# A linear-attention and two-MLP kernel with its order set by its own list scheduler: heads on one half of the rows, weight words two tiles at a time, ten token tiles run ahead

## The chip, the cores and the metric

One core of a Trainium2 chip runs the whole program. The metric is the device time of one execution in microseconds, from the first to the last instruction and what lies around them. Engines: PE (TensorE, with its weight loads as PEld), DVE (VectorE), ACT (ScalarE), POOL (GpSimd), and SP, which here only issues transfers.

## The reference

The inputs are `q`, `k`, `v` of (4, 8, 768, 64) in float32. Per batch and head a state of 64x64 decays by gamma and takes up `k v` at each of the 768 positions; the output is the query times the state. The outputs, as 3072 tokens of 512, go through two MLPs. The weights are float64.

```python
for t in range(S):
    state = gamma[None, :, None, None] * state + einsum('bhd,bhe->bhde', k[:, :, t], v[:, :, t])
    y[:, :, t] = scale * einsum('bhd,bhde->bhe', q[:, :, t], state)
x = y.transpose(0, 2, 1, 3).reshape(B * S, H * D)          # (3072, 512)
h = x @ w_in                                               # d_ff 1024
e = exp(h - max(h)); sm = e / (sum(e) + 1e-9); s = h * sm
ln = (s - mean(s)) / sqrt(var(s) + 1e-6) * g_ln
x = ln @ w_out                                             # (3072, 512)
h = x @ w_in2                                              # d_ff 2048
out = (h * cos(h)) @ w_out2
```

## The kernel before

**Attention** runs in 24 steps (two batch pairs of 12 chunks of 64 positions). A step makes one token tile of 128 rows by 512. `score_pair` (lines 230, 231) multiplies keys by queries, `score_mask` (L248) applies the decayed mask in two halves of 64 rows, `state_pair` (L241) adds to the 64x64 states in PSUM, `state_copy` (L255, L256) copies them to SBUF, and `att_out` (L287, L290) multiplies scores and queries, laid one above the other on 128 rows, by values and state, then scales into `x`. Scores and state run with K=64 on quadrants of the array, outputs with K=128 and 64 columns. `att_prep` has POOL scale the mask (L219) and ACT the keys (L223). Each step's loads are six transfers on SP's queue (L91 to L98).

**Words.** A float64 weight is read as two int32 words; `load_w` (L155 to L167) makes a float32 of them, a tile of 128x512 at a time: one ACT operation and four of DVE. `load_w1` and `load_o1` do it for the first MLP, `keep` does it for the second and stores the result (L191), `load_kept` fetches it again (L195). Every matmul operand is split into a high part and a residual (`split`, L125 on ACT, L128 on DVE), and a product is three matmuls.

**First MLP.** Per tile `mm1` (L315) makes two halves of 12 matmuls of 512 columns; `norm` (L323 to L336) does the softmax and the normalization, its small operations on DVE and one power on POOL (L334). Per pair of tiles `transp` (L351) transposes in four groups, with L354 and L355 for high part and residual, and `mm2` (L368) makes 2 x 48 matmuls of 256 columns; its result goes to DRAM (`y1d`).

**Second MLP.** Per block of 512 tokens and per j of 16, `up` (L393) makes 12 matmuls of 512 columns, then ACT and DVE work out `h cos(h)` (L400 to L405, L125, L128), and `down` (L418) adds 12 matmuls into four accumulators, `LAG` = 3 later. L423 copies them out and L427 stores them.

**Order.** PE's order is as written (`manual_schedule` for PE alone); the other engines' order is made by the framework's own timeline. At the start the loads of `w_in`, steps 0 to 3 of the attention and the first halves of `mm1` are interleaved by hand. Then `EARLY` = 2 groups, that is four token tiles, run ahead of the loop over 256-token groups, in which each turn has two tiles of `mm1`, one group of `transp` and `mm2`, attention steps (`att_both`, where scores of step n+1 and state of step n alternate) and some `weights`. Only from that loop on do scores and state alternate; before, they are blocks of their own.

Of the kernel before, what the change touches and what calls it, by code (L numbers as in the profile page):

```python
# [22 lines left out]
C = 64  # L23
# [9 lines left out]
K2 = FF2 // 128  # L33
NG = NT // 256
NBLK = NT // 512
LAG = 3
EARLY = 2
RING = 6
TINY = float(np.array([0x38100000], np.uint32).view(np.float32)[0])
# [8 lines left out]


@with_exitstack  # L50
def body(ctx: ExitStack, tc: tile.TileContext, qx, kt, kn, vn, c_sc, c_mg,
         w_in1, w_out1, gln, w_in2, w_out2, out):
    nc = tc.nc
    pe_order = tc.manual_schedule(engines={mybir.EngineType.PE})
    ctx.enter_context(pe_order)

    const = ctx.enter_context(tc.tile_pool(name="const", bufs=1, side="left"))
    dram = ctx.enter_context(tc.tile_pool(name="dram", bufs=1, space=DRAM))
    p_hp = ctx.enter_context(tc.tile_pool(name="hp", bufs=1, side="right"))
    hp = p_hp.tile([128, 120], F32, name="hp")  # L60
    p_w2a = ctx.enter_context(tc.tile_pool(name="w2a", bufs=1, side="right"))
    stg = ctx.enter_context(tc.tile_pool(name="stg", bufs=2, side="right"))

    y1d = [dram.tile([128, KD, 512], F32, name=f"y1d{n}") for n in range(NBLK)]


    ph1 = ExitStack()
    p_w1 = ctx.enter_context(tc.tile_pool(name="w1", bufs=1, side="left", reuse_waits="tile"))
    p_u = ctx.enter_context(tc.tile_pool(name="u", bufs=2 * EARLY + 2, side="left", reuse_waits="tile"))
    moe = ph1.enter_context(tc.tile_pool(name="moe", bufs=1, side="left", reuse_waits="tile"))  # L70
    boot = ExitStack()
    boot_w = ExitStack()
    p_boot = boot_w.enter_context(tc.tile_pool(name="boot", bufs=1, side="left", reuse_waits="tile"))
    ps1 = ph1.enter_context(tc.tile_pool(name="ps1", bufs=1, side="left", space=PSUM))
    att = ExitStack()
    pa = att.enter_context(tc.tile_pool(name="att", bufs=3, side="right", reuse_waits="tile"))
    psa = att.enter_context(tc.tile_pool(name="psa", bufs=1, side="right", space=PSUM))


    steps = [(bp, i) for bp in range(NB2) for i in range(NI)]  # L80
    st = {}

    def load_step(n):
        bp, i = steps[n]
        d = {}
        d["kt"] = pa.tile([128, 8, C], F32, tag="kt", name="kt", bufs=2)
        d["X"] = pa.tile([128, 2, 8, C], F32, tag="X", name="X")
        d["kn"] = pa.tile([128, NHP, 2 * D], F32, tag="kn", name="kn")
        d["W"] = pa.tile([128, 2, 8, D], F32, tag="W", name="W")
        d["mg"] = pa.tile([128, 2, NHP, C], F32, tag="mg", name="mg", bufs=2)  # L90
        nc.sync.dma_start(out=d["kt"], in_=kt[bp, i].rearrange("p (j s) -> p j s", s=C))  # L91
        src = qx[bp, i].rearrange("p (j s) -> p j s", s=C)
        nc.sync.dma_start(out=d["X"][64:128, 0], in_=src[64:128])
        nc.sync.dma_start(out=d["X"][0:64, 1], in_=src[0:64])
        src = vn[bp, i].rearrange("p (j s) -> p j s", s=D)
        nc.sync.dma_start(out=d["W"][0:64, 0], in_=src[0:64])
        nc.sync.dma_start(out=d["W"][64:128, 1], in_=src[64:128])
        nc.sync.dma_start(out=d["kn"], in_=kn[bp, i].rearrange("p (j s) -> p j s", s=2 * D))  # L98
        if i == 0:
            nc.gpsimd.memset(d["W"][64:128, 0], 0.0)  # L100
            nc.gpsimd.memset(d["W"][0:64, 1], 0.0)
        st[n] = d

    load_step(0)
    mg = const.tile([128, 2, NHP, C], F32, name="mg")
    cs = const.tile([128, 3, NI, NHP], F32, name="cs")
    gcol = const.tile([128, K1], F32, name="gcol")
    nc.scalar.dma_start(out=mg, in_=c_mg.rearrange("p (u a t) -> p u a t", u=2, t=C))
    nc.scalar.dma_start(out=cs, in_=c_sc.rearrange("p (u a t) -> p u a t", u=3, t=NHP))
    nc.scalar.dma_start(out=gcol, in_=gln)  # L110
    mhalf = const.tile([128, 1], F32, name="mhalf")
    nc.gpsimd.memset(mhalf, -0.5)
    nc.gpsimd.memset(hp[:, 0:1], HALFPI)
    sms = [const.tile([128, 16], F32, name=f"sm{n}") for n in range(3)]
    const.tile([128, 16], F32, name="pad")
    ident = const.tile([128, 128], F32, name="ident")
    make_identity(nc, ident)


    w1h = p_w1.tile([128, KD, FF1], F32R, tag="w1h", name="w1h")  # L120
    w1l = p_w1.tile([128, KD, FF1], F32R, tag="w1l", name="w1l")
    o1 = []

    def split(hi, lo, src, pin=False, head=None):
        op = nc.scalar.activation(out=hi, in_=src if head is None else head, func=AF.Copy)  # L125
        if pin:
            tc.keep_in_program_order(op)
        nc.vector.tensor_tensor(out=lo, in0=src, in1=hi.bitcast(F32), op=ALU.subtract)  # L128

    p2 = {}  # L130
    seq = [0]

    early = []

    def fetch_w1(c):
        for k in range(KD):
            raw = p_boot.tile([128, 512, 2], I32, tag="raw", name="raw", bufs=2 * KD)
            nc.sync.dma_start(
                out=raw, in_=w_in1[k * 128:(k + 1) * 128, c * 1024:(c + 1) * 1024].rearrange("p (f two) -> p f two", two=2))
            early.append(raw)  # L140

    def load_w(src, apart=False):
        seq[0] += 1
        if early:
            raw = early.pop(0)
            src = None
            t = p_boot.tile([128, 512], I32, tag="wt", name="wt", bufs=4)
        elif "lt" not in p2 and seq[0] % 2:
            raw = p2["boot"].tile([128, 512, 2], I32, tag="raw", name="raw", bufs=3)
            t = p2["boot"].tile([128, 512], I32, tag="wt", name="wt", bufs=2)  # L150
        else:
            raw = stg.tile([128, 512, 2], I32, tag="raw", name="raw", bufs=3)
            t = stg.tile([128, 512], I32, tag="wt", name="wt")
        if src is not None:
            nc.sync.dma_start(out=raw, in_=src.rearrange("p (f two) -> p f two", two=2))  # L155
        f = t.bitcast(F32)
        top, low = raw[:, :, 1], raw[:, :, 0]
        first_op = nc.scalar.activation(out=f, in_=top.bitcast(F32), func=AF.Abs)
        if seq[0] > 2 * KD:
            tc.keep_in_program_order(first_op)  # L160
        nc.vector.tensor_scalar(out=f, in0=f, scalar1=TINY, scalar2=HUGE, op0=ALU.max, op1=ALU.min)  # L161
        nc.vector.tensor_scalar(out=t, in0=t, scalar1=3, scalar2=0x3FFFFFFF,  # L162
                                op0=ALU.logical_shift_left, op1=ALU.bitwise_and)
        nc.vector.scalar_tensor_tensor(out=t, in0=top, scalar=-0x40000000, in1=t,  # L164
                                       op0=ALU.bitwise_and, op1=ALU.bitwise_or)
        full = low if apart else t
        nc.vector.scalar_tensor_tensor(out=full, in0=low, scalar=29, in1=t,  # L167
                                       op0=ALU.logical_shift_right, op1=ALU.bitwise_or)
        return (f, full.bitcast(F32)) if apart else f

    w_in1, w_out1, w_in2, w_out2 = (w.bitcast(I32) for w in (w_in1, w_out1, w_in2, w_out2))

    def load_w1(k, c):
        head, t = load_w(w_in1[k * 128:(k + 1) * 128, c * 1024:(c + 1) * 1024], True)
        cs = slice(c * 512, (c + 1) * 512)
        split(w1h[:, k, cs], w1l[:, k, cs], t, head=head)

    def load_o1(j):
        head, t = load_w(w_out1[j * 128:(j + 1) * 128, :], True)
        nc.scalar.activation(out=o1[0][:, j], in_=head, func=AF.Copy, scale=gcol[:, j:j + 1])  # L180
        nc.vector.scalar_tensor_tensor(
            out=o1[1][:, j], in0=t, scalar=gcol[:, j:j + 1], in1=o1[0][:, j].bitcast(F32),
            op0=ALU.mult, op1=ALU.subtract)

    w2h, w2l = {}, {}
    kept = {}

    def keep(kind, c, e, k, src):
        if k == 0:
            kept[kind, c, e] = dram.tile([128, 2, 512], F32, name=f"kept_{kind}_{c}_{e}")  # L190
        nc.sync.dma_start(out=kept[kind, c, e][:, k], in_=load_w(src))  # L191

    def load_kept(what, hi, lo):
        t = stg.tile([128, 2, 512], F32, tag="raw", name="raw", bufs=3)
        nc.sync.dma_start(out=t, in_=kept[what])  # L195
# [471 lines left out]
```

## Time and profile before

| | us |
|---|---|
| Time, median of 3 runs | 934.29 |
| Lowest and highest | 926.18 and 934.35 |
| Span of the profiled execution | 932.8 |

The profile is of one execution, of 932.8 us from its first to its last instruction; the median is 1.5 us longer. Engine rows give busy time; PE's ends are modelled, so matmuls that overlap count as one busy stretch. The granted clock (PEclk) is the share of TensorE's full clock, 1.0 or 0.5 at any one moment, averaged over a stretch. A wait is put down to what ended it.

### The profile page before, as it was taken

How to read it: one execution, taken by the hardware profiler on the slowest of the kernel's cores; microseconds unless marked ns; L12 is line 12 of the kernel's file. 1: busy time of each engine (PE TensorE's matmuls, PEld its weight loads, DVE VectorE, ACT ScalarE, POOL GpSimd, SP SyncE). 2: the span in 40 equal slices, each digit the busy share in tenths (PEclk: the TensorE clock that was granted, in tenths of full speed). 3: DMA queues.
4: the chain of work that ended last, by engine and by line, in shares of the span. 5: the costliest groups of instructions: out<-in, count | busy, mean ns of one | idle time of the engine just before them, and what ended most of it. 6: DMA issues, size and time to landing. Idle time of an engine off the chain costs nothing.

```text
span 932.8 us, 16044 instructions
## 1 busy us (share of the span) xinstructions
PE 893.4 (96%) x6464; PEld 765.1 (82%) x6464; DVE 622.7 (67%) x1090; ACT 455.5 (49%) x768; POOL 48.0 (5%) x60
## 2 busy tenths in 40 slices
PE   4787999989899999999999999999999999999997
PEld 4676889879799989998888888888888888888886
DVE  6899887587667754566766655756575665656654
ACT  4677666556656555554534333433443343344332
POOL 2112100101011000000000000000000000000000
PEclk7999899989999999999999999999999999999999
DMA  9986354565547422133012002000300030001001
GB/s 260 313 252 194 106 158 146 184 204 161 188 131 226 157 93 90 64 108 111 24 35 56 1 1 73 19 0 1 91 1 1 7 84 1 1 24 45 1 1 46
DMA packets 41884, 85.28 MB, mean 91 GB/s; under 512 B 5457, under 2 KB 11729, under 8 KB 41809
## 3 DMA queue, kind: packets, MB, share of 16 engines
q1 hardware_dynamic: 41376, 83.91, 30.0%
q8 instruction: 51, 0.84, 0.4%
q10 hardware_dynamic: 432, 0.34, 0.1%
q14 instruction: 25, 0.20, 0.1%
HBM read 64.30 MB, written 19.92 MB: 90 GB/s over the span
## 4 chain that ended last, share of the span: by engine, by line
PE 84%; DVE 6%; DMA 5%; ACT 2%; issue 2%; SPq 1%; POOL 0%; DVEq 0%; ACTq 0%
PE h L393 28%; PE acc L418 28%; PE y L368 13%; PE h L315 10%; DMA kn<-kn_dram 3%; PE tr L351 2%; PE y L287 2%; DMA W<-vn_dram 1%; PE sc L230 1%; DVE X L248 1%; DVE wt L164 1%; DVE wt L161 1%; ACT kn L223 1%; ACT junk L328 1%; DVE wt L162 0%
## 5 line engine op out<-in xcount | busy, mean ns | idle before, releaser
L393 PE MATMUL h<-yh,w2h 128*128 128x512 f32 x384 | 149.6, 390 | 0.0
L393 PE MATMUL h<-yl,w2h 128*128 128x512 f32 x384 | 149.4, 389 | 0.0
L393 PE MATMUL h<-yh,w2l 128*128 128x512 f32 x384 | 149.4, 389 | 0.0
L418 PE MATMUL acc<-o2h,gh 128*128 128x512 f32 x384 | 149.4, 389 | 0.0
L418 PE MATMUL acc<-o2h,gl 128*128 128x512 f32 x384 | 149.4, 389 | 0.0
L418 PE MATMUL acc<-o2l,gh 128*128 128x512 f32 x384 | 149.4, 389 | 0.0
L404 ACT ACTIVATE r<-r,hp 128x512 f32<-128x512 f32 x96 | 69.5, 724 | 144.5 <-DVE r L403 144.5
L368 PE MATMUL y<-lth,o1h 128*128 128x256 f32 x384 | 110.2, 287 | 0.0
L368 PE MATMUL y<-ltl,o1h 128*128 128x256 f32 x384 | 108.8, 283 | 0.0
L368 PE MATMUL y<-lth,o1l 128*128 128x256 f32 x384 | 108.6, 283 | 0.0
L401 DVE SCALAR_TENSOR_TENSOR r<-ki,h 128x512 f32<-128x512 int32 x96 | 66.0, 687 | 62.9 <-ACT ki L400 61.9
L405 DVE TENSOR_TENSOR r<-r,h 128x512 f32<-128x512 f32 x96 | 66.0, 687 | 61.6 <-ACT r L404 61.6
L128 DVE TENSOR_TENSOR gl<-r,gh 128x512 fp32r<-128x512 f32 x96 | 66.3, 691 | 45.9 <-ACT gh L125 45.4
L400 ACT ACTIVATE ki<-h 128x512 int32<-128x512 f32 x96 | 57.3, 597 | 74.7 <-PE h L393 74.1
L125 ACT ACTIVATE gh<-r 128x512 fp32r<-128x512 f32 x96 | 60.7, 632 | 65.4 <-DVE r L405 65.4
L393 PEld LDWEIGHTS h<-yh,w2h 128*128 128x128 f32 x384 | 72.1, 188 | 14.9
L418 PEld LDWEIGHTS acc<-o2h,gl 128*128 128x128 f32 x384 | 72.1, 188 | 15.0
L393 PEld LDWEIGHTS h<-yl,w2h 128*128 128x128 f32 x384 | 72.1, 188 | 15.0
L418 PEld LDWEIGHTS acc<-o2l,gh 128*128 128x128 f32 x384 | 72.1, 188 | 14.9
L418 PEld LDWEIGHTS acc<-o2h,gh 128*128 128x128 f32 x384 | 72.0, 188 | 14.9
L393 PEld LDWEIGHTS h<-yh,w2l 128*128 128x128 f32 x384 | 72.1, 188 | 14.8
L315 PE MATMUL h<-w1h,xh 128*128 128x512 f32 x192 | 77.9, 406 | 0.0
(77 smaller groups left out, 1554.3 us busy)
## 6 DMA issues: line engine op xcount, KB each, us to landing
raw<-w_in_dram SPq DMA_DIRECT2D x24, 512.0 KB, 4.4
raw<-w_out_dram SPq DMA_DIRECT2D x24, 512.0 KB, 4.8
kt<-kt_dram SPq DMA_DIRECT2D x24, 256.0 KB, 4.9
X<-qx_dram SPq DMA_DIRECT2D x48, 128.0 KB, 5.0
W<-vn_dram SPq DMA_DIRECT2D x48, 128.0 KB, 4.6
kn<-kn_dram SPq DMA_DIRECT2D x24, 256.0 KB, 5.1
y1d<-ys SPq DMA_DIRECT2D x24, 256.0 KB, 2.1
yt<-y1d SPq DMA_DIRECT2D x24, 256.0 KB, 2.9
```

The source lines that it names most:

```text
L125: op = nc.scalar.activation(out=hi, in_=src if head is None else head, func=AF.Copy)
L128: nc.vector.tensor_tensor(out=lo, in0=src, in1=hi.bitcast(F32), op=ALU.subtract)
L287: nc.tensor.matmul(out=y[64 * par:64 * par + 64, j], lhsT=d["W"][:, par, j], rhs=d["X"][:, par, j], start=True, stop=True)
L315: nc.tensor.matmul(out=h[:, c], lhsT=a[:, k], rhs=w[:, k, cs], start=(k + m == 0), stop=(k == KD - 1 and m == 2))
L351: nc.tensor.transpose(out=tr[:, e, t * 128:(t + 1) * 128], in_=lns[2 * g + t].rearrange("p c f -> p (c f)")[:, j * 128:(j + 1) * 128], ide ...
L368: nc.tensor.matmul(out=y1[:, e], lhsT=w[:, j, ds], rhs=a[:, j % 2], start=(m == 0), stop=(m == 3 * K1 - 1))
L393: nc.tensor.matmul(out=h, lhsT=w[:, k, cs], rhs=a[:, k], start=(m == 0), stop=(m == 3 * KD - 1))
L400: nc.scalar.activation(out=ki, in_=h, func=AF.Identity, scale=INV2PI, bias=0.25)
L401: nc.vector.scalar_tensor_tensor(out=r, in0=ki, scalar=-C1, in1=h, op0=ALU.mult, op1=ALU.add)
L404: nc.scalar.activation(out=r, in_=r, func=AF.Sin, bias=hp[:, 0:1])
L405: nc.vector.tensor_tensor(out=r, in0=r, in1=h, op=ALU.mult)
L418: nc.tensor.matmul(out=acc, lhsT=a[:, ts_], rhs=w, start=(j == 0 and m == 0), stop=(j == K2 - 1 and m == 2))
```

## The change

A class `Plan` takes every operation of every engine with an estimated cost, what it reads and writes, and a due time: the PE cost recorded so far plus a bias. Its `order` goes through all of them by earliest possible start (PE within `LOOK` = 4 of its written order, SP within a window of due times, the others by due time), and the instructions are issued in that order on all engines.

Keys and queries of a step come in one transfer, values and keys in another, and the row scaling in a third; the keys' scaling by position moves from ACT to the values on POOL, the mask is a plain triangle, and the decay goes into the output's scaling. A head stays on its half of the 128 rows: scores and state on the diagonal quadrants of the array, outputs as two products of K=64 on the other two. Rows of `w_in` are turned to match. `words` treats two tiles at once (128x1024), except for the first two tiles. The small operations of a norm are on POOL. `EARLY` is 5: ten tiles of `mm1` and `norm` run before the first `mm2`, in `NU` = 10 buffers; the first weights of the second MLP are kept in DRAM like the others. Between, the 20 halves of ten groups are spread over 14 tiles, the last two groups lie beside `up` as before. `up` and `down` have the same instructions and order on PE.

```diff
-EARLY = 2
+EARLY = 5
+NU = 10
 RING = 6
+REST = 2
...
+MBUS = 0.29
+LAND = 2.0
+LOOK = 4
...
+SP_WIN = 6.0
+B_STORE = 10.0
+B_YS = 6.0
+B_LOAD = 0.0
...
+class Plan:
...
+        self.ops.append((eng, cost, fn, deps, mb, look, name, self.clock + bias))
+        if eng == "PE":
+            self.clock += cost
...
+    def order(self):
...
+                    cand = [i for i in pe[at:at + ops[pe[at]][5]] if not left[i] and not done[i]]
+                elif e == "SP":
+                    while sat < len(sp) and done[sp[sat]]:
+                        sat += 1
+                    if sat == len(sp):
+                        continue
+                    cand = [i for i in sp[sat:sat + 8 + stuck] if not left[i] and not done[i]
+                            and (stuck or ops[i][7] <= ops[sp[sat]][7] + SP_WIN)]
...
+                start = max(free[e], min(ready[i] for i in cand))
+                cand = [i for i in cand if ready[i] <= start]
+                i = min(cand) if e == "PE" else min(cand, key=lambda i: (ops[i][7], i))
+                if best is None or start < best[0]:
+                    best = (start, e, i)
...
+    def run(self):
+        for i in self.order():
+            self.ops[i][2]()
...
+        self.add("SP", 0.45, dk, r=[("pool", "att")], w=[("dk", sl)], mb=0.524, bias=B_LOAD)
+        self.add("SP", 0.45, sv, r=[("pool", "att")], w=[("v", sl), ("kn", sl)], mb=0.524, bias=B_LOAD)
+        self.add("SP", 0.45, g, r=[("pool", "att")], w=[("g", sl)], mb=0.131, bias=B_LOAD)
+        def scale():
+            v = self.t["sv", n][:, 0].rearrange("p (a b) e -> p a (b e)", b=2)
+            self.nc.gpsimd.tensor_tensor(out=v, in0=v, in1=self.kf[:, i].unsqueeze(2).to_broadcast([128, NHP, 2 * D]),
+                                         op=ALU.mult)
+        self.add("POOL", 1.12, scale, w=[("v", sl)])
...
+        for r in self.half:
+            self.nc.tensor.matmul(out=sc[r, j], lhsT=dk[r, 0, j], rhs=dk[r, 1, j], start=True, stop=True)
...
+        for r in self.half:
+            self.nc.tensor.matmul(out=sp[r, j], lhsT=sv[r, 1, j], rhs=sv[r, 0, j],
+                                  start=(i == 0 and j == 0), stop=(i == NI - 2 and j == 7), skip_group_check=True)
...
+        for p in range(2):
+            r = self.half[p]
+            if intra:
+                lhs, rhs = self.t["sv", n][r, 0, j], self.t["M", n][r, j]
+            else:
+                lhs, rhs = self.t["s", n][r, j], self.t["dk", n][r, 1, j]
+            self.nc.tensor.matmul(out=self.t["y", n][self.half[1 - p], j], lhsT=lhs, rhs=rhs,
+                                  start=(intra and j == 0), stop=(j == 7 and last), skip_group_check=True)
...
+            two += [(self.out_pair, n, intra, j) for intra in ((True, False) if i else (True,)) for j in range(8)]
+        def go():
+            for k in range(max(len(one), len(two))):
+                for q in (one, two):
+                    if k < len(q):
+                        q[k][0](*q[k][1:])
...
+                self.nc.vector.tensor_tensor(out=m, in0=self.t["sc", scores],
+                                             in1=self.tri.unsqueeze(1).to_broadcast([128, 8, C]), op=ALU.mult)
...
+        self.add("SP", 0.5, fetch, r=[("pool", pool)], w=[rk], mb=0.5245 * wide, bias=b)
+        self.add("ACT", 0.1 + 0.53 * wide, top, r=[rk], w=[wk], bias=b)
+        self.add("DVE", 0.17 + 0.28 * wide, clamp, w=[wk], bias=b)
+        self.add("DVE", 0.17 + 0.28 * wide, shift, w=[wk], bias=b)
+        self.add("DVE", 0.15 + 0.55 * wide, sign, r=[rk], w=[wk], bias=b)
+        self.add("DVE", 0.15 + 0.55 * wide, low, r=[wk] if apart else [rk], w=[rk] if apart else [wk], bias=b)
+        return rk, wk
...
+        def p1():
+            self.nc.gpsimd.tensor_scalar(out=sm[:, 5:6], in0=sm[:, 1:2], scalar1=1e-9, scalar2=None, op0=ALU.add)
+            self.nc.gpsimd.tensor_tensor(out=sm[:, 6:7], in0=sm[:, 5:6], in1=sm[:, 5:6], op=ALU.mult)
+            self.nc.gpsimd.tensor_scalar(out=sm[:, 6:7], in0=sm[:, 6:7], scalar1=1e-6, scalar2=None, op0=ALU.mult)
+        def p2():
+            self.nc.gpsimd.tensor_scalar(out=sm[:, 3:4], in0=sm[:, 2:3], scalar1=-1.0 / FF1, scalar2=None, op0=ALU.mult)
+        def n4():
+            junk = self.new("moe", ("junk", n), [128, 2, 512], BF16, "junk")
+            self.nc.scalar.activation(out=junk, in_=T["u", n], func=AF.Square, bias=sm[:, 3:4], accum_out=sm[:, 4:5])
+        def p3():
+            self.nc.gpsimd.tensor_scalar(out=sm[:, 7:8], in0=sm[:, 4:5], scalar1=1.0 / FF1, scalar2=sm[:, 6:7],
+                                         op0=ALU.mult, op1=ALU.add)
+            self.nc.gpsimd.tensor_tensor(out=sm[:, 8:9], in0=sm[:, 7:8], in1=self.mhalf, op=ALU.pow)
+            self.nc.gpsimd.tensor_tensor(out=sm[:, 9:10], in0=sm[:, 3:4], in1=sm[:, 8:9], op=ALU.mult)
+        def n5():
+            self.nc.scalar.activation(out=T["u", n], in_=T["u", n], func=AF.Identity, scale=sm[:, 8:9], bias=sm[:, 9:10])
...
+        self.w1(0, 0, 1, 0)
+        self.load(0)
+        self.w1(0, 1, 1, 1)
+        self.attn(scores=0, look=look)
+        self.load(1)
+        self.w1(0, 2, 2, 2)
+        self.attn(outs=0, look=look)
+        self.attn(scores=1, look=look)
+        self.load(2)
+        self.attn(outs=1, look=look)
+        self.w1(1, 0, 2, 3)
...
+        self.mm1(0, 0, ((0,), (1,), (2, 3)), look=look)
+        attend()
+        self.mm1(1, 0, look=look)
+        self.w1(1, 2, 2, 4)
+        attend()
...
+        for n in range(1, 2 * EARLY):
+            if n > 1:
+                self.mm1(n, 0, look=look)
+            for _ in range(O1_AT.count(n)):
+                self.o1(*oq.pop(0))
+            self.mm1(n, 1, look=look)
+            attend()
...
+        halves = [(g, p) for g in range(NG - REST) for p in range(2)]
+        rest = NS - 2 * EARLY
+        for m, n in enumerate(range(2 * EARLY, NS)):
+            mine = halves[m * len(halves) // rest:(m + 1) * len(halves) // rest]
+            after = mine[-1:]
+            for g, p in mine[:-1]:
+                if p == 0:
+                    for f in range(4):
+                        self.transp(g, f, look=look)
+                self.mm1(n, 0, look=look)
+                self.mm2(g, p, look=look)
+                keep()
+            g, p = after[0]
+            if p == 0:
+                self.transp(g, 0, look=look)
+                self.transp(g, 1, look=look)
+            if len(mine) == 1:
+                self.mm1(n, 0, look=look)
+            if p == 0 and len(mine) == 1:
+                self.transp(g, 2, look=look)
+                self.transp(g, 3, look=look)
+            self.mm1(n, 1, look=look)
+            if p == 0 and len(mine) > 1:
+                self.transp(g, 2, look=look)
+                self.transp(g, 3, look=look)
+            attend()
+            self.mm2(g, p, look=look)
+            keep()
...
```

## Rows read from the trace of the kernel before

**Rows 1.** The page, part 1: busy us, share of the span, instructions.
```profile
PE 893.4 (96%) x6464; PEld 765.1 (82%) x6464; DVE 622.7 (67%) x1090; ACT 455.5 (49%) x768; POOL 48.0 (5%) x60
```

**Rows 2.** By stage: length, busy us of each engine, granted clock, DMA share, GB/s.
```profile
0.00:40.00 40.00, 22.99 (x339) 19.67 (x340) 27.81 (x49) 21.82 (x45) 6.92 (x15) 0.83 0.99 286
40.00:60.00 20.00, 19.22 (x331) 16.06 (x329) 18.65 (x33) 15.20 (x31) 3.91 (x4) 1.00 0.88 257
60.00:100.00 40.00, 30.88 (x455) 25.69 (x455) 39.30 (x72) 29.20 (x57) 9.95 (x10) 0.91 0.65 182
100.00:260.00 160.00, 152.30 (x1690) 137.07 (x1689) 117.88 (x234) 96.67 (x169) 17.48 (x20) 0.98 0.55 170
260.00:900.00 640.00, 640.00 (x3534) 543.74 (x3533) 403.88 (x680) 283.13 (x453) 9.78 (x13) 1.00 0.17 52
900.00:933.00 33.00, 28.00 (x124) 22.86 (x122) 15.14 (x25) 9.50 (x17) 0.00 (x0) 0.99 0.14 33
```

**Rows 3.** Waits of PE: us in total, times, longest us.
```profile
PE tr L351 <- DVE ltl L355: 7.6, 5, 4.1
```

**Rows 4.** Pieces of the chain that ended last: start us, us, what.
```profile
99.98 0.87 PE tr L351 x8
...
133.48 5.95 PE y L368 x48
...
144.90 5.75 PE y L368 x48
150.65 2.75 PE h L315 x12
...
552.64 2.72 PE acc L418 x12
```

**Rows 5.** Timeline of PE, one attention step: start us, us, what, records.
```profile
219.97 0.27 PE L230 MATMUL sc<-X,kt 64*64 64x64 f32 x1
219.98 0.27 PE L231 MATMUL sc<-X,kt 64*64 64x64 f32 x1
219.98 0.27 PE L241 MATMUL S<-W,kn 64*64 64x64 f32 x2
...
220.09 0.23 PE L241 MATMUL S<-W,kn 64*64 64x64 f32 x2
...
220.91 0.23 PE L241 MATMUL S<-W,kn 64*64 64x64 f32 x2
221.06 1.15 PE L287 MATMUL y<-X,W 128*64 128x64 f32 x32
222.14 0.39 PE L368 MATMUL y<-lth,o1h 128*128 128x256 f32 x1
```

**Rows 6.** Groups by line and shape: busy us, mean ns; then idle before.
```profile
L164 DVE SCALAR_TENSOR_TENSOR wt<-raw,wt 128x512 int32<-128x512 int32 x48 | 33.0, 688 | 0.8
...
L325 DVE SCALAR_TENSOR_TENSOR u<-u,h 128x1024 f32<-128x1024 f32 x24 | 29.3, 1220 | 5.4 <-ACT u L324 4.9
...
L162 DVE TENSOR_SCALAR wt<-wt 128x512 int32<-128x512 int32 x48 | 23.1, 485 | 0.7
...
L334 POOL TENSOR_TENSOR sm<-sm,mhalf 128x1 f32<-128x1 f32 x24 | 17.8, 743 | 119.9 <-DVE sm L332 119.9
...
L290 DVE TENSOR_TENSOR x<-y,mg 128x512 f32<-128x512 f32 x24 | 16.5, 687 | 0.4
...
L167 DVE SCALAR_TENSOR_TENSOR raw<-raw,wt 128x512 int32<-128x512 int32 x16 | 13.5, 847 | 0.1
```

**Rows 7.** Timeline of DVE and POOL near 28 us.
```profile
27.96 1.60 DVE L161 TENSOR_SCALAR wt<-wt 128x512 f32<-128x512 f32 x2
...
28.19 1.09 POOL L219 TENSOR_TENSOR mg<-mg,cs 128x512 f32<-128x512 f32 x1 [11.15 <-DVE x L290]
```

**Rows 8.** What SP's queue waited for (us, times, longest), and one load's time to landing.
```profile
SPq L191 <- DVE wt L167: 74.9, 24, 9.0
...
X<-qx_dram SPq DMA_DIRECT2D x48, 128.0 KB, 5.0
```

More of the change, by code (lines that the diff above doesn't have):

```diff
@@ L33 @@
 K2 = FF2 // 128
+NS = NB2 * NI
 NG = NT // 256
@@ new lines, with __init__, add @@
+HOP = 0.12
+MBUS = 0.29
+LAND = 2.0
+LOOK = 4
+B_W1 = 0.0
+B_O1 = 16.0
+B_KEEP = 12.0
+B_BACK = 2.0
+B_UP = 4.0
+O1_AT = (1, 2, 4, 5)
+SP_WIN = 6.0
[3 more added lines that the diff above has]
+class Plan:
+    def __init__(self):
+        self.ops = []
+        self.last = {}
+        self.readers = {}
+        self.clock = 0.0
+    def add(self, eng, cost, fn, r=(), w=(), mb=0.0, look=1, bias=0.0, name=""):
+        i = len(self.ops)
+        deps = set()
+        for k in r:
+            if k in self.last:
+                deps.add(self.last[k])
+        for k in w:
+            if k in self.last:
+                deps.add(self.last[k])
+            deps.update(self.readers.get(k, ()))
+        for k in r:
+            self.readers.setdefault(k, []).append(i)
+        for k in w:
+            self.last[k] = i
+            self.readers[k] = []
+        deps.discard(i)
+        self.ops.append((eng, cost, fn, deps, mb, look, name, self.clock + bias))
+        if eng == "PE":
+            self.clock += cost
+    def order(self):
+        ops = self.ops
+        n = len(ops)
+        succ = [[] for _ in ops]
+        for i, o in enumerate(ops):
+            for d in o[3]:
+                succ[d].append(i)
+        engines = ("CTL", "PE", "DVE", "ACT", "POOL", "SP")
+        free = {e: 0.0 for e in engines}
+        free["SP"] = free["ACT"] = free["DVE"] = 1.0
+        wire = 2.0
+        left = [len(o[3]) for o in ops]
+        ready = [0.0] * n
+        avail = {e: [] for e in engines}
+        for i, o in enumerate(ops):
+            if not left[i]:
+                avail[o[0]].append(i)
+        pe = [i for i, o in enumerate(ops) if o[0] == "PE"]
+        sp = sorted((i for i, o in enumerate(ops) if o[0] == "SP"), key=lambda i: (ops[i][7], i))
+        at, sat, out = 0, 0, []
+        done = [False] * n
+        self.times = [None] * n
+        stuck = 0
+        while len(out) < n:
+            best = None
+            for e in engines:
+                if e == "PE":
+                    while at < len(pe) and done[pe[at]]:
+                        at += 1
+                    if at == len(pe):
+                        continue
[4 more added lines that the diff above has]
+                    if sat == len(sp):
+                        continue
+                    cand = [i for i in sp[sat:sat + 8 + stuck] if not left[i] and not done[i]
+                            and (stuck or ops[i][7] <= ops[sp[sat]][7] + SP_WIN)]
+                else:
+                    cand = avail[e]
+                if not cand:
+                    continue
+                start = max(free[e], min(ready[i] for i in cand))
[3 more added lines that the diff above has]
+                    best = (start, e, i)
+            if best is None:
+                stuck += 1
+                continue
+            stuck = 0
+            start, e, i = best
+            if e not in ("PE", "SP"):
+                avail[e].remove(i)
+            done[i] = True
+            out.append(i)
+            end = start + ops[i][1]
+            free[e] = end
+            self.times[i] = (start, end)
+            if ops[i][4]:
+                wire = max(wire, end) + ops[i][4] / MBUS
+                end = wire + LAND
+            for s in succ[i]:
+                hop = 0.0 if ops[s][0] == e and not ops[i][4] or e == "CTL" else HOP
+                ready[s] = max(ready[s], end + hop)
+                left[s] -= 1
+                if not left[s] and ops[s][0] not in ("PE", "SP"):
+                    avail[ops[s][0]].append(s)
+        return out
+    def run(self):
+        for i in self.order():
+            self.ops[i][2]()
@@ L604, with body @@
+@with_exitstack
+def body(ctx: ExitStack, tc: tile.TileContext, kq, vk, c_g, c_tri, c_kf, w_in1, w_out1, gln, w_in2, w_out2, out):
+    b = Body(ctx, tc, kq=kq, vk=vk, c_g=c_g, c_tri=c_tri, c_kf=c_kf, w_in1=w_in1, w_out1=w_out1, gln=gln,
+             w_in2=w_in2, w_out2=w_out2, out=out)
+    b.setup()
+    b.record()
+    b.plan.run()
+    for name in ("psacc", "psh", "sb", "wo", "stg", "u", "w1"):
+        b.shut(name)
 _OUTS = [((NT, DM), "float32")]
@@ L655 @@
     ]
-    nc = bacc.Bacc("TRN2", target_bir_lowering=False, num_devices=1)
+    nc = bacc.Bacc("TRN2", target_bir_lowering=False, num_devices=1, dynamic_dma_scratch_size=4096)
     arrays, args = {}, []
```

1077 lines of the change are left out of this document (562 added, 515 removed).

## The prediction

> **What bounds the kernel now.** I read the busy shares first: TensorE 96% [rows 1]. So the program is already close to its matmuls, and the question is which microseconds of the span are not matmul work at full clock. The table by stage says where they are [rows 2]: in 0 to 40 us PE is busy 22.99, in 40 to 60 19.22, in 60 to 100 30.88, together 26.9 us idle out of 100; in 100 to 260 another 7.7; then nothing up to 900 (640.00 busy); at the end 5 us (28.00 of 33.00) for the last copies and stores. The granted clock falls in the same stretches, 0.83, 0.91 and 0.98, since after a pause PE works at the lower of its two levels. In 40 to 100 us VectorE is busy 57.95 of 60 us, in 0 to 40 the DMA share is 0.99: the start is bound by transfers, then by DVE. The list of waits [rows 3] gives the later pauses: transposes that wait for DVE's residuals, five times, 7.6 us in all, the longest 4.1.
>
> Now the work itself, from the chain's pieces [rows 4]. `up` and `down` are 192 pieces of 12 matmuls, 2.72 us each: 522.2. `mm1` is 48 half tiles of 12, 2.75: 132.0. `mm2` is 24 pieces of 48, 5.75 to 5.95, say 5.85: 140.4. Eight transposes are a piece of 0.87: 24 times that is 20.9. An attention step of the late kind begins at 219.97 and the next matmul starts at 222.14 [rows 5], 2.17 us; in the early nine steps scores, state and outputs are three separate blocks, which by the same rounds come to 0.95 + 0.95 + 1.15 and the handoffs, some 3.2: 15 x 2.17 + 9 x 3.2 = 61.4. Sum 876.9. With 5.3 us before the first matmul and 5 at the end, 45.6 of the 932.8 are left: 29.3 of idle time inside (34.6 less the first 5.3), the rest half clock and handoffs.
>
> **The change part by part.** The matmuls of `up`, `down`, `mm1`, `mm2` and the transposes stay as they are: 815.5 us that nothing here touches. What can move is the attention, the pauses and the clock.
>
> **Attention on PE.** A step now has 64 products of 64x64 (outputs split in two products of K=64) in place of 48 of which 16 have K=128. They go out as 16 slots, each one pair on the diagonal quadrants of the array (scores, state) and one pair on the other two (outputs). A product makes two records. In [rows 5] four records, L230, L231 and two of L241, start within 0.01 us; the second such round has its L241 at 220.09 and the sixteenth at 220.91, 14 rounds of 0.058 each. So four quadrants work at once. Then a step is 32 rounds x 0.058 = 1.86, with 0.11 to enter and some 0.1 to leave 2.05; 24 steps 49.2 in place of 61.4: 12.2 gained. Bounds: 1.86 at best (44.6), and without overlap of the two kinds of pair twice the rounds, 3.71 + 0.2 = 3.9 (94). I take 2.05, the row is of the same shape.
> The Trainium skill (TensorE: Matmul & The Clock Gate, section "Part 3: Packing small matmuls — row/col tiling") says that a weight load goes beside a matmul in flight only where its row group is another one. By that the two kinds of pair, which share their rows, would follow each other, and the sum would be some 45 us higher; the trace does not agree for scores beside state, which share rows too.
>
> **Pauses after 100 us.** Ten token tiles instead of four run ahead of the transposes, some 75 us of PE work between a norm and its reader, so the waits of [rows 3] go: 7.7 us idle, and with them the half clock (160 x 0.02 = 3.2). Gain 10.9. The cover is that distance; what is late next is the release of the single score buffer after a norm (exponential and product, 2.4 us of DVE and as much ScalarE), which lies under 5.85 us of `mm2`. Between 0 and 0.5 us for each of 14 tiles are 0 to 7; I put 2 us for all such handoffs, nearer to the pause-free stretch after 260 us.
>
> **The start.** Here DVE decides, so I count its work up to the first `mm1` of tile 10, from [rows 6]. Attention and split: 14 masks (now one of 128 rows for two of 64), 13 outputs, 11 residuals, 38 x 0.69 = 26.2. Norms of tiles 0 to 8, reduce and product: 18 x 1.22 = 22.0; the small DVE operations of a norm go to POOL. Words two tiles at a time: the two one-source steps are not in the trace at 1024 columns; below, 0.485 and nothing added would be 0.49, above twice 0.485 = 0.97; I take 0.75 (0.485 and half of the 0.53 that 512 more columns cost L325 over L164). The sign step is 1.22 (L325's shape). The low step into the raw tile, 0.847 in the rows, lies between 1.22 and 1.69: 1.4. A pair is 4.1; for w_in with its residual 5.3, for w_out with two scaled residuals 5.5. Four pairs of each: 43.2. Sum 91.4.
> POOL is dearer to DVE: in [rows 7] two one-source word steps, of the kind that averages 0.48, take 1.60 together while POOL multiplies for 1.09 beside them, so a meeting costs some 0.6. 13 scalings of V and the norms' powers fall into this stretch; half of the 16 word steps meeting one is 16 x 0.5 x 0.5 = 4. Bounds: 0, and the 14 us that 13 scalings of 1.09 last.
> DVE starts with the first raw tile, about 6 us. It then waits for transfers: the last words of w_in1 are the end of the first 8.9 MB (4.2 and four steps of 1.18), which takes 31 us at 286 GB/s [rows 2] and has landed by 33; in the 27 us until then DVE has 22 us of work (three pairs, nine steps of 0.69): 5 lost. With 3% of small gaps (39.30 of 40 busy in [rows 2] is 2%) DVE is at that point at 6 + 5 + 91.4 + 4 + 3 = 109.4. PE alone would be there sooner: the last pair of w_in1 is done at 33 + 1.2 + 5.3, near 40, PE has by then done 3.5 half tiles and four steps, 18 us, and the rest of 20 half tiles and 13 steps (55.0 + 26.7 = 81.7) brings it to 103. So DVE ends last: 109.4.
> From there PE has 815.5 + 49.2 - 81.7 = 783.0, and 5 at the end: 897.4, with 2 for handoffs 899.4. By differences: 932.8 - 12.2 - 10.9 = 909.7, so the start gives 10 of the up to 32 us (21.6 idle, 10 of clock) that it loses now.
>
> **What costs nothing.** Seven small POOL operations of a norm are not in the trace: between nothing and L334's 0.74 [rows 6] each, at most 5.2 us for a tile, with V's scaling of 1.09 no more than 6.3, less than the 7.5 us of PE work per tile; nobody reads a norm for ten tiles. ScalarE loses four scalings and one of two state copies a step. Transfers per step grow from 1.02 to 1.18 MB, with a DMA share of 0.65 and 0.55 in the stages after 60 us. SP's order is now fixed beforehand, stores and loads in one queue; a load goes out when the step before the last has freed its buffer, 13 us before its use (5.5 + 2.05 + 5.5), and lands in 5, so a store ahead of it may wait 8 us; [rows 8] show 74.9 us in 24 waits, 3.1 each, 9.0 the longest. The change of stages at 380 us and the last stage keep their order and their two to four buffers: PE is 100% busy there now, so nothing is to be gained, and an `up` chain on DVE and ACT of 6 us has 16 us until its `down`.
>
> The sum is against the profiled span of 932.8; the median 934.3 is 1.5 above it (one run was 8 below). So 899.4 + 1.5, about 901.
>
> **The rivals.** (a) Transfers and PE, not DVE, end the start: PE reaches tile 10 at 103, span 891, time 892. For it: a step's DVE share falls from three instructions of 0.69 to two; against it: 57.95 of 60 us busy. (b) POOL holds DVE for the whole of V's scalings, 14 us in place of 4, and the start gives nothing: 901 + 10 = 911. For it: [rows 7]; against it: L164 and L290, with two inputs each, average 0.69 over the whole program [rows 6], and POOL worked beside some of them.
> The Trainium skill (SBUF — State Buffer, section "SBUF: two separate sides") states this as a rule, an exclusive lock of a port that both engines share, for the whole instruction; [rows 7] agree for the one-source steps.
> (c) The two kinds of pair don't overlap: the attention is 94, not 49, and the time 946; the change would then not do what it says. [rows 5] speak against it. (d) Slower: on SP's queue stores block loads. From 3.0 us of lateness in each of the 11 attention steps that lie beside `mm2`, the whole gain of 33 is gone; at 4 us each the time is 945. That asks for waits of 11 us, over the longest of [rows 8], each time.
>
> **How the numbers follow.** Forecast 0.42, (a) 0.22, (b) 0.20, (c) 0.03, (d) 0.04, and 0.09 for a lesser mishap of a fixed order, in which most of the gain is lost. Range 887 to 920: (a) with 5 us below, (b) with 9 above. A change of 1% is about what can be told from none. Faster by more than that (below 925): 0.42 + 0.22 + 0.20 and 0.04 of the last case, 0.88; within 1% 0.05; slower by over 1% 0.07.
>
> **What would show it.** Right: `mm1` of tile 10 starts near 110 us with DVE over 95% busy from 40 to there; one attention step takes 2.0 to 2.1 us with rounds of 0.058; no pause over 1 us of PE from 115 to 895, granted clock 1.00. Wrong: rounds of 0.116 (c); word steps over 1.2 us in most cases (b); PE idle before scores or outputs with a DMA as releaser after 110 us (d); any pause in the last stage.

## The result, and the profile after

The changed kernel takes 898.67 us (median of 4 runs, 897.74 to 900.29) and the kernel before, beside it, 930.23 (926.15 to 934.35): a ratio of 0.9652, 95% interval 0.9606 to 0.9698. The profiled execution spans 898.5 us in place of 932.8. The page, part 1, answers to [rows 1]:

```profile
PE 876.3 (98%) x7168; PEld 751.6 (84%) x7168; DVE 580.6 (65%) x849; ACT 408.7 (45%) x630; POOL 100.1 (11%) x200
```

PE's busy time fell by 17.1 us, though it has 704 records more; the other half of the 34.3 is idle time. By stage, with the columns of [rows 2] (the second row, 10 to 20, lies inside the first):

```profile
0.00:40.00 40.00, 23.96 (x545) 19.71 (x546) 29.25 (x36) 13.71 (x17) 8.56 (x14) 0.96 0.84 307
10.00:20.00 10.00, 7.51 (x192) 6.97 (x187) 6.29 (x11) 4.08 (x6) 2.31 (x2) 0.83 1.03 407
40.00:60.00 20.00, 19.57 (x316) 15.97 (x316) 16.00 (x22) 13.28 (x21) 9.18 (x20) 0.91 0.66 234
60.00:100.00 40.00, 40.00 (x795) 32.99 (x796) 37.81 (x48) 30.20 (x45) 20.16 (x37) 1.00 0.61 203
100.00:260.00 160.00, 159.39 (x2248) 145.71 (x2240) 109.45 (x141) 84.11 (x127) 46.20 (x93) 1.00 0.60 202
260.00:900.00 640.00, 633.34 (x3283) 537.21 (x3281) 388.07 (x605) 267.36 (x424) 16.00 (x38) 1.00 0.17 51
```

Idle PE in the first 100 us is 16.5 us (26.9 before), in 100 to 260 it is 0.6 (7.7 before), and the clock is at its full level from 60 us on. From 260 to the end at 898.5 are 638.5 us, of which PE is busy 633.3: the last stage lost nothing, and its 5 us at the end are those of before. The whole list of PE's waits (us in total, times, longest) no longer has the transposes of [rows 3]:

```profile
PE sc L257 <- DMA dk<-kq_dram: 7.0, 1, 7.0
PE h L471 <- DVE w1l L401: 4.5, 3, 1.9
PE y L278 <- DVE M L311: 2.0, 1, 2.0
PE h L471 <- ACT w1h L398: 1.4, 1, 1.4
PE S L265 <- POOL sv L246: 1.1, 2, 0.6
PE y L561 <- issue: 0.5, 1, 0.5
PE h L471 <- DVE u L493: 0.4, 1, 0.4
```

After the first load the largest wait is that of `mm1` for the residuals of w_in1's words, 4.5 us, all before 40 us. The chain that ended last shows the same place (start us, us, what):

```profile
...
38.22 1.47 DVE w1l L401
...
39.74 5.54 PE h L471 x16
45.30 1.12 DVE sm L487
46.44 1.23 DVE u L493 x2
...
47.72 5.73 PE h L471 x24
...
55.48 5.67 PE h L471 x24
...
88.86 1.21 DVE u L493 x2
...
101.64 0.09 DVE u L493
...
101.78 5.73 PE h L471 x24
```

DVE stands in the chain up to the residual that ends at 39.7 and once more at 45.3 to 47.7; from 47.7 a tile's `mm1` begins every 7.69 us, 5.67 for itself and 2.03 for an attention step. From 88.9 to 101.7 the chain runs through DVE again: `mm1` of tile 9 begins 7.91 us behind that of tile 8, 0.2 later than the pace. When the same kernel was timed again (below), this step was 7.70 and PE alone set it. The two engines are that close there. `mm1` of tile 10 begins at 109.45, forecast 109.4. A step on PE's timeline (start us, us, what, records), to hold against [rows 5]:

```profile
130.34 0.27 PE L257 MATMUL sc<-dk 64*64 64x64 f32 x2
130.35 0.27 PE L278 MATMUL y<-M,sv 64*64 64x64 f32 x2
130.45 0.23 PE L257 MATMUL sc<-dk 64*64 64x64 f32 x2
130.46 0.22 PE L278 MATMUL y<-M,sv 64*64 64x64 f32 x2
130.51 0.22 PE L257 MATMUL sc<-dk 64*64 64x64 f32 x2
130.52 0.23 PE L278 MATMUL y<-M,sv 64*64 64x64 f32 x2
```

Two scores and two outputs start within 0.01 us of each other. The second four start 0.11 us later, and from there a round of four comes every 0.06. The first matmul behind the step starts at 132.37, so the step takes 2.03. DVE and POOL by line and shape (busy us, mean ns; then idle before):

```profile
L366 DVE SCALAR_TENSOR_TENSOR wt<-raw,wt 128x1024 int32<-128x1024 int32 x23 | 31.2, 1355 | 0.7
...
L357 DVE TENSOR_SCALAR wt<-wt 128x1024 f32<-128x1024 f32 x23 | 16.7, 727 | 6.9 <-ACT wt L353 6.8
...
L361 DVE TENSOR_SCALAR wt<-wt 128x1024 int32<-128x1024 int32 x23 | 15.9, 693 | 0.6
...
L373 DVE SCALAR_TENSOR_TENSOR raw<-raw,wt 128x1024 int32<-128x1024 int32 x7 | 8.6, 1225 | 0.2
...
L246 POOL TENSOR_TENSOR sv<-sv,kf 128x512 f32<-128x512 f32 x24 | 26.7, 1111 | 90.8 <-DMA sv<-vk_dram 81.7 <-PE h L471 7.8 <-PE tr L533 1.3
```

The wide one-source steps (L357, L361) take 0.69 to 0.73, the low step (L373) 1.23. L366, whose work is like L373's, has a mean of 1.36, and the timeline of DVE and POOL shows where that comes from (start us, us, what):

```profile
27.16 1.30 POOL L246 TENSOR_TENSOR sv<-sv,kf 128x512 f32<-128x512 f32 x1 [7.48 <-DMA sv<-vk_dram]
27.60 1.95 DVE L366 SCALAR_TENSOR_TENSOR wt<-raw,wt 128x1024 int32<-128x1024 int32 x1
29.58 1.23 DVE L373 SCALAR_TENSOR_TENSOR raw<-raw,wt 128x1024 int32<-128x1024 int32 x1
29.93 1.78 POOL L246 TENSOR_TENSOR sv<-sv,kf 128x512 f32<-128x512 f32 x1 [1.46 <-DMA sv<-vk_dram]
30.72 1.53 DVE L357 TENSOR_SCALAR wt<-wt 128x1024 f32<-128x1024 f32 x1
```

Beside POOL's scaling of V, L366 took 1.95 and L357 1.53; alone they take 1.22 and 0.69. Of the 23 instructions of L366, the four that began while POOL scaled V took 1.94 to 2.06, the others 1.22 to 1.23. Where DVE began first the delay fell on POOL: L373 at 29.58 kept its 1.23, and the scaling beside it took 1.78, against a mean of 1.11.

### The profile page after: what moved, and what is told of

It is laid out like the page before. It is cut to its first block, busy times and chain, and to the rows that moved or that the text cites. A ratio compares the mean times of both kernels' runs of the same rounds, so it can differ in the third digit from the quotient of the medians.

```text
span 898.5 us, 16993 instructions
## 1 busy us (share of the span) xinstructions
PE 876.3 (98%) x7168; PEld 751.6 (84%) x7168; DVE 580.6 (65%) x849; ACT 408.7 (45%) x630; POOL 100.1 (11%) x200
## 4 chain that ended last, share of the span: by engine, by line
PE 93%; DVE 4%; DMA 1%; issue 1%; ACT 0%; POOL 0%; SPq 0%; DVEq 0%; POOLq 0%
PE h L671 29%; PE acc L732 29%; PE y L561 16%; PE h L471 13%; PE tr L533 2%; PE sc L257 1%; PE y L278 1%; PE S L265 1%; DVE wt L366 1%; DMA sv<-vk_dram 1%; DVE raw L373 1%; DVE w1l L401 0%; DVE wt L357 0%; DVE wt L361 0%; DVE u L493 0%
## 5 line engine op out<-in xcount | busy, mean ns | idle before, releaser
L732 PEld LDWEIGHTS acc<-o2h,gl 128*128 128x128 f32 x384 | 72.1, 188 | 14.9
```

Of the source, the lines that this page charges most:

```text
L732: nc.tensor.matmul(out=T["acc", n, t], lhsT=a[:, ts_], rhs=w, start=(j == 0 and m == 0), stop=(j == K2 - 1 and m == 2))
```

## The experiments

Each is the changed kernel with one edit (the last with one more on top). The changed kernel itself was timed again beside the last two and the planned order on PE alone:

> The changed kernel as it is, beside the next ones on one chip, since they may differ from it by 1 or 2 us. 897 to 900.

It took 898.93 us (898.08 to 899.31), ratio to before 0.9656 [0.9630, 0.9682], with tile 10 at 109.42.

**Scores, state and outputs as blocks.**

```diff
-            for k in range(max(len(one), len(two))):
-                for q in (one, two):
-                    if k < len(q):
-                        q[k][0](*q[k][1:])
+            for q in (one, two):
+                for step in q:
+                    step[0](*step[1:])
```

> Theory: the attention step is short because a pair on the diagonal quadrants and a pair on the other two run at once. With all of scores and state first and all outputs behind them, only two quadrants work at a time: 64 rounds of 0.058 us in place of 32, a step of 3.8 to 3.9 us in place of 2.03, 24 steps some 44 us more, time about 940 (898.7 + 44 less a few us where a step lies beside the waits of the start). Rival: PE's rate is set by records issued, not by quadrants, and a step keeps its 2.0 us: no change, 899.

928.55 us, ratio 0.9970 [0.9952, 0.9989]: nearly all the gain is gone. One step on PE's timeline:

```profile
166.73 1.15 PE L257 MATMUL sc<-dk 64*64 64x64 f32 x32
167.71 0.93 PE L265 MATMUL S<-sv 64*64 64x64 f32 x26
```

The 32 records of scores go out from 166.73 to 167.71, in rounds of two at the same 0.06 us each; a step is now 64 such rounds, 3.71 us, and not 32 rounds of four, 2.03. Of 24 x 1.68 = 40 us, 30 came out: tile 10 began at 121.5, 12 us later and not 22, because the longer steps fill the start's waits for words (`mm1` of tile 2 began at 48.28, only 0.6 later). What the four quadrants at once save is thus the size of the whole change; in two pairs one after the other, 64 products are dearer than the 48 of before.

**Four tiles ahead, as before, instead of ten.**

```diff
-EARLY = 5
+EARLY = 2
...
-O1_AT = (1, 2, 4, 5)
+O1_AT = (1, 1, 2, 3)
```

> Four token tiles ahead of the first transposes in place of ten, the planner free to order anew, w_out1's words spread over tiles 1 to 3. Theory: the distance buys DVE time. Until the first mm2 DVE then has 43 us of words, 17 steps of attention and split of 0.69 and norms of four tiles, some 66 us and 5 for POOL's company, done near 80 us, while PE's work up to there would be done near 70: PE waits 8 to 15 us there, time 907 to 914. Rival: the planned order alone keeps PE fed, the ten tiles are worth nothing: 899 to 901.

910.61 us, ratio 0.9784 [0.9754, 0.9814]. PE's waits have the transposes again:

```profile
PE tr L533 <- DVE ltl L544: 5.3, 1, 5.3
...
PE tr L533 <- DVE u L493: 2.8, 1, 2.8
PE h L471 <- DVE u L493: 1.9, 2, 1.5
```

The distance of ten tiles is worth 12 us: 10.0 of these waits, and 1.7 for the half clock that follows them here from 76.6 to 80.0.

**The order in which the program states its operations, instead of the list scheduler's.**

```diff
-        for i in self.order():
+        for i in range(len(self.ops)):
```

> The plan's order is left out: every engine gets its instructions in the order in which they are recorded. Theory: the list scheduler's part is to put DVE's small urgent steps (mask, output, split) between the word steps; without it a mask stands behind whole word groups of 4 to 5 us, on PE some 8 attention steps at the start wait that long, and SP issues loads no earlier than written. The start loses 20 us or more and pauses come back after 100 us: 920 to 950. Rival: the written order is good already, and the planner adds nothing that can be measured: 899 to 903.

1210.92 us, ratio 1.3037 [1.2995, 1.3078], far beyond what was expected. PE's waits, then SP's queue's:

```profile
PE tr L533 <- DVE ltl L544: 96.0, 11, 13.1
PE sc L257 <- DMA dk<-kq_dram: 87.3, 8, 14.9
```
```profile
...
SPq L575 <- ACT ys L570: 304.6, 22, 26.3
SPq L431 <- DVE wt L373: 165.5, 16, 11.0
```

On SP's queue stores of `ys` and of kept words stand ahead of the loads of a later step, and PE waits 87 us for `dk`. The longest of these waits shows how: a store of kept words (L431), which had waited for its words, goes out at 246.41 us, the load of `dk` right behind it at 246.84, and PE waits 14.9 us until 251.62. In the changed kernel the same two rows of SP's queue are not small either, and cost PE nothing:

```profile
SPq L575 <- ACT ys L570: 133.1, 24, 14.1
...
SPq L431 <- DVE wt L373: 63.7, 10, 12.1
```

So the mechanism of rival (d) is real. The plan gives a store a later due time than a load (`B_STORE`, `B_YS` against `B_LOAD`), which would keep it away; that was not tried by itself. The edit alters DVE's and ScalarE's order as well (the 96 us of transposes), so SP's share of the 312 us is not separated.

**The planned order on PE alone, the other engines left to the framework's scheduling as before.**

```diff
-        ctx.enter_context(tc.manual_schedule())
+        ctx.enter_context(tc.manual_schedule(engines={mybir.EngineType.PE}))
```

> PE's order as planned, but the order of all other engines is left to the framework's timeline, as in the kernel before; the plan's order is only where it starts from. Theory: what the plan adds over the framework is mainly SP's and DVE's due times; with the framework's priorities the start is late by some us and a few pauses come back, 905 to 925. Rival: the framework finds as good an order, 897 to 901, and the list scheduler for the other engines is worth nothing.

968.85 us, ratio 1.0416 [1.0381, 1.0450]. A wait of PE, and one stage (columns as above):

```profile
PE y L278 <- DVE x L324: 17.2, 5, 5.8
```
```profile
60.00:120.00 60.00, 44.26 (x629) 36.23 (x630) 47.65 (x60) 29.51 (x40) 26.34 (x40) 0.76 0.78 271
```

DVE is busy only 47.65 of 60 us there and yet late. Word steps stand ahead of the attention's output (L324), and they in turn wait for raw words: DVE idles 10.5 us before L357 in this stretch. PE idles 15.7 of 60 us, with a clock of 0.76. Without the planned order on every engine the other parts make the kernel 4% slower than before.

**DVE more loaded before and after 40 us.** The clamp of w_in1's words done twice (below with the key "w1"), or of w_out1's ("o1"):

```diff
+            if key[0] == "w1":
+                self.nc.vector.tensor_scalar(out=f, in0=f, scalar1=TINY, scalar2=HUGE, op0=ALU.max, op1=ALU.min)
```

> The clamp of each word tile of w_in1 is done twice, in the same planned order: 2 x 0.43 + 3 x 0.69 = 2.9 us more DVE work before 45 us. Theory (DVE decides until w_in1's words are done, PE sets the pace from there): mm1 of tile 10 starts 2.9 us later, near 112.4, time +2.9, about 901.6. Rival 1 (transfers decide the first 45 us): less than 1 us later. Rival 2 (DVE decides all the way to tile 10): +2.9 as well; the run with w_out1's clamps tells it from the theory.

> The clamp of each word tile of w_out1 is done twice, in the same planned order: 4 x 0.69 = 2.8 us more DVE work between 45 and 100 us. Theory (PE sets the pace from 47.7 us, DVE has a few us in hand): mm1 of tile 10 still starts within 1 us of 109.45, time 898 to 900. Rival (DVE decides all the way to tile 10, as predicted): 2.8 us later, time about 901.5.

For w_in1 900.52 us, ratio 0.9682 [0.9655, 0.9709], tile 10 at 110.02; for w_out1 899.20, 0.9662 [0.9638, 0.9687], tile 10 at 108.57. These intervals hold neither time apart from the changed kernel's. The starts of tile 10 cannot be compared without the clock. From 40 to 46 us (columns as above), first the changed kernel, then w_out1's clamps, then the run with V scaled by ScalarE further below:

```profile
40.00:46.00 6.00, 6.00 (x68) 4.61 (x71) 2.81 (x4) 2.53 (x5) 0.66 (x3) 0.72 0.97 366
...
40.00:46.00 6.00, 5.69 (x144) 4.62 (x143) 4.41 (x7) 4.14 (x6) 0.65 (x3) 1.00 0.96 365
...
40.00:46.00 6.00, 5.57 (x144) 4.58 (x143) 5.08 (x8) 4.93 (x8) 1.36 (x5) 1.00 1.03 416
```

With w_out1's clamps the program up to there is that of the changed kernel, and the wait before is the same (1.42 and 1.41 us), but the half clock behind it is missing. So `mm1` of tile 2 begins at 46.12 and not 47.72: 1.6 us that no clamp gave. From tile 2 to tile 10 it then takes 62.45 us, against 61.73 in the changed kernel and 61.55 when that was timed again. Of the 2.8 us (4 x 0.69) of work put on DVE 0.7 to 0.9 came out, nearly all just ahead of tile 9. DVE does not pace that whole stretch, but it has only some 2 us in hand in it.

With w_in1's clamps (clock 1.00 from 40 to 46 us as well) PE's last wait for a residual ended at 42.02, against 39.87 in the changed kernel timed again: 2.2 us later, for 2.9 us of work. Tile 10 was only 0.6 later, because the half clock lay before 34 us. By tile 10 alone the rival (transfers decide the start) would seem right; the residual shows that DVE's word steps set its time.

**The norm's small operations on DVE again, the power staying on POOL.**

```diff
-            self.nc.gpsimd.tensor_scalar(out=sm[:, 5:6], in0=sm[:, 1:2], scalar1=1e-9, scalar2=None, op0=ALU.add)
+            self.nc.vector.tensor_scalar(out=sm[:, 5:6], in0=sm[:, 1:2], scalar1=1e-9, scalar2=None, op0=ALU.add)
...
-        self.add("POOL", 0.25, p2, w=[sk])
+        self.add("DVE", 0.15, p2, w=[sk])
```

> A norm's small operations, all but the power, are on DVE again, five of 0.15 to 0.2 us per tile, ordered anew. Theory: 1.0 us more DVE per tile, 9 us by tile 10, against some 6 us that DVE has in hand there; PE waits 2 to 5 us before tile 10, time 901 to 904. Rival: POOL's small operations hold up DVE as much as they save (word steps beside them are longer), so the move was worth nothing: 898 to 900.

905.06 us, ratio 0.9743 [0.9713, 0.9773], tile 10 at 115.51. One line of PE's waits is new:

```profile
PE sc L257 <- DVE M L311: 3.1, 2, 2.9
```

Half clock from 101.9 to 108.7 follows it. The move to POOL is worth 6 us, most of it where DVE was near a tie with PE.

**Words one tile at a time**, for w_in1 and w_out1:

```diff
...
-        self.w1(0, 2, 2, 2)
+        self.w1(0, 2, 1, 2)
+        self.w1(0, 3, 1, 3)
...
```

> Words of w_in1 and w_out1 one tile at a time (twice the instructions, 0.43 for 0.69 and 0.69 for 1.22 us); what is kept for the second MLP stays at two. By the durations a pair costs 0.17 + 0.17 + 0.16 + 0.16 + 0.14 = 0.8 us more DVE; three pairs of w_in1 2.4 us, and w_out1 0.7 each, within DVE's reserve. Theory (DVE decides until w_in1 is done): tile 10 some 2 us later, time about 901, unless tiles that come ready sooner give it back. Rival: single tiles let mm1 start on each as it comes, and the wide form costs latency: 897 to 898, faster.

900.45 us, ratio 0.9692 [0.9663, 0.9722], tile 10 at 109.42: no difference that can be told.

**V's scaling left out** (the values go unscaled into the state and the outputs; the order is planned anew):

```diff
...
-        self.add("POOL", 1.12, scale, w=[("v", sl)])
+        self.add("CTL", 0.0, scale, w=[("v", sl)])
```

> V's scaling on POOL is left out (the values go unscaled into state and outputs). Theory: POOL's 1.1 us multiplication lengthens the DVE steps that meet it; in the first 45 us four such steps are 0.71, 0.73, 0.84 and 0.24 us longer than their kind, 2.5 us in all, so tile 10 starts 2 to 3 us earlier, time about 896. Rival: the longer steps lie in DVE's idle time or PE's waits and nothing changes: 898 to 899.

900.10 us, ratio 0.9691 [0.9662, 0.9720], tile 10 at 109.41: the 2 to 3 us expected did not come. The plan moved with it: the second tile's `mm1` began at 36.47 and not 31.57, half clock lay at 25.9 to 32.7, and PE's last wait for a residual ended at 41.51, later than the 39.87 of the changed kernel. So it does not tell what POOL's company costs.

**V of the first five steps scaled by ScalarE**, which is busy 13.71 of the first 40 us:

```diff
...
+            for a in range(NHP):
+                self.nc.scalar.activation(out=v[:, a], in_=v[:, a], func=AF.Copy, scale=self.kf[:, i, a:a + 1])
+        if n < 5:
+            self.add("ACT", 1.35, scale_act, w=[("v", sl)])
...
```

> V of the first five steps is scaled by ACT in four pieces (4 x 0.39 us, as the keys were before) and not by POOL, ordered anew. Theory: POOL beside DVE lengthens DVE's one-source steps and a few others in the first 45 us by some 2.5 us in all, and DVE decides there; ACT has 26 of the first 40 us free: tile 10 up to 2 us earlier, time 896 to 898. Rival: the lengthened steps are covered by waits for transfers or PE and nothing is gained, 898 to 900.

896.29 us (895.64 to 898.60), ratio 0.9631 [0.9607, 0.9656], tile 10 at 105.84: 3.6 us sooner than in the changed kernel timed again. Not all of that is POOL's. PE's last wait for a residual ended at 37.92 and not 39.87, 1.9 us sooner. The other 1.6 are the half clock from 40 to 46 us, which this execution does not have (rows above): its own, at 16.1 to 19.5 and 26.3 to 29.7, lay where PE still waits for words. DVE's timeline (here L365 and L374 are L357 and L366):

```profile
25.26 0.68 DVE L365 TENSOR_SCALAR wt<-wt 128x1024 f32<-128x1024 f32 x1
...
26.70 1.23 DVE L374 SCALAR_TENSOR_TENSOR wt<-raw,wt 128x1024 int32<-128x1024 int32 x1
```

Without POOL beside it, no word step of DVE was lengthened before 40 us, and PE's wait for w_in1's residuals fell from 4.5 to 2.4. This is the best version measured, by 2.6 us in the medians; the two intervals of the ratio still overlap, so that it is faster is likely and not shown.

**That, and w_in1's three wide residuals on POOL.**

```diff
-            self.nc.vector.tensor_tensor(out=self.w1l[:, ks, cs], in0=self.t["full", key],
+            (self.nc.gpsimd if wide > 1 else self.nc.vector).tensor_tensor(out=self.w1l[:, ks, cs], in0=self.t["full", key],
...
```

> As the run before, and the residuals of w_in1's three wide word tiles are on POOL (3 x 1.22 to 1.46 us of DVE less in the first 45 us). Theory (DVE decides there): another 2 to 3 us earlier, time 893 to 896, faster than both kernels. Rival: POOL takes more than 2 us for such a residual and the last of them is what mm1 waits for, so it gives nothing or costs 1 to 2 us: 897 to 901.

898.36 us, ratio 0.9654 [0.9630, 0.9678], tile 10 at 109.11. PE's longest wait after the first load now names POOL:

```profile
PE h L479 <- POOL w1l L409: 2.7, 2, 2.3
```

The subtraction takes 2.42 to 2.75 us there and 1.22 on DVE, and it is what PE waits for; the last such wait ends at 39.95 and not 37.92. What DVE was spared came back.

## Why the prediction was right, and where it was not

- **Attention.** Forecast 2.05 us a step, measured 2.03, and the blocks at 3.71 by the upper bound's working (3.9). Rival (c) fell. The Trainium skill (TensorE: Matmul & The Clock Gate, section "Part 3: Packing small matmuls — row/col tiling") would have had the pairs that share rows follow each other; the rounds of 0.06 us for four records show that here they did not.
- **Pauses after 100 us.** Forecast gone, and they are: 0.6 us idle in 100 to 260, clock 1.00. With four tiles ahead they came back. The 2 us put down for handoffs were not found in idle time; from tile 10 to the end it took 789.0 us, forecast 783.0 + 5 + 2 = 790.
- **The start: time right, cause partly wrong.** The step that failed is "So DVE ends last: 109.4", with "PE alone" at 103. The sign named for it, DVE over 95% busy from 40 us to tile 10, did not appear: 16.00 of 20 us, then 37.81 of 40, while PE had 40.00 of 40. DVE ends last up to the last words of w_in1, done at 39.7 (forecast "near 40"), and its norm holds PE for 0.4 us more at 47.7. From there PE sets the pace, and DVE is near a tie with it: 0.2 us late ahead of tile 9 in one execution, not late in another, 0.7 to 0.9 with 2.8 us more to do, and 6 with the norm's operations put back on it. Rival (a) thus had the right engine for that stretch and, at 103, the wrong time; transfers were not what ended the part before it.
- **The terms that were mis-sized.** PE's 103 was too low: at 39.7 it had done 2.7 half tiles, not 3.5 (2.2 us); a tile's `mm1` takes 5.67 between attention steps and not 5.50 (17.3 half tiles, 1.5 us); it ran at half clock from 40.5 to 44.0, after the wait for the residual (1.7 us, a cost that other executions did not have); one step took 2.52 (0.5). With these PE stands at 109. DVE's 109.4 was too high: a wide one-source step is 0.69, not 0.75, and the low step 1.23, not 1.4; DVE was busy 90.8 us up to tile 10, not 95.4. Two errors of opposite sign met: that 109.45 came so near 109.4 is luck.
- **POOL beside DVE.** In (b) the two-input groups L164 and L290 were held against it. The new L366, with two inputs, went from 1.22 to 1.95 beside POOL, so that argument was too weak; L290 reads one of its two from PSUM. With the scaling on ScalarE the last residual came 1.9 us sooner and the median was 2.6 lower, with intervals that overlap: a price of about 2 us at the start, not the 10 of (b). The Trainium skill (SBUF — State Buffer, section "SBUF: two separate sides") describes one port that DVE or POOL holds for a whole instruction, whichever starts first, and counts DVE's instructions with two inputs in SBUF among those that need it. The 1.95 and 1.53 beside POOL agree, and so do L373's 1.23 with the 1.78 of POOL behind it; the mask and output products (L311, L324), of whose two inputs one lies in PSUM, keep 0.68 to 0.69 beside POOL.
- **The last stage and the loads.** Both cost nothing, as said. The planned order, though, is more than a carrier: left to PE alone it turns 32 us of gain into 38 of loss. The prediction gave that no term.
- **The sum.** Of the 34.3 us of span, attention gives 61.4 - 24 x 2.03 = 12.7 (the 61.4 is the prediction's own estimate), idle time after 100 us 7.1 and idle time before it 10.4. The rest, 4, would be the clock, which was not measured by itself. That is against the profiled span; the prediction of 901 is 2.3 above the median.

## What to carry to other kernels

Small products that fill only a part of the TensorE array, here 64x64 in float32, are worth issuing as interleaved pairs on the other quadrants; hold the rounds in PE's timeline against a block to see whether they go side by side. Running a producer's stage many tiles ahead removes both waits and the half clock behind them, but here only with the other engines' queues ordered for it too (969 us without). Compare two executions by the end of one wait before comparing a later start: half clock that falls at another place moved such a start by 1.6 us. When two engines end a stage within a few per cent of each other, work out both from the trace and call it a tie: a right sum does not show which of them decides.

## What the runs showed of the hardware that was not expected

In 10 to 20 us the core moved 407 GB/s (the second row by stage above). The kernel before, in the same stretch:

```profile
10.00:20.00 10.00, 3.60 (x64) 3.11 (x62) 9.61 (x18) 5.05 (x10) 1.35 (x1) 0.69 1.04 271
```

The DMA share is the same, 1.03 and 1.04. Raw words now come in transfers of 1024 KB, not 512, and keys and values in 512 KB, not 128 and 256; which of these matters was not tried. POOL's power (L511) took 0.89 us in place of 0.74 [rows 6], and its other operations on 128x1 between 0.19 and 0.58. The half clock after a pause does not come out alike: behind the same wait it was there or not, and `mm1` of tile 2 began between 46.1 and 47.9 us in executions whose program was the same up to there.
